# Conv 2's row terms in a tile of their own, added by an accumulating DMA, and its end rows evicted by ScalarE

## The chip, the cores and the metric

The kernel runs on one core of one Trainium2 chip. The metric is the device time of one execution in microseconds (us), as the median of several runs. Below, PE is the matrix engine (TensorE), PEld its weight load, DVE is VectorE, ACT is ScalarE, POOL is GpSimd and SP is SyncE. Each engine works through its own queue of instructions in order. DMAs are issued from the queues of SP (plain loads and stores) and POOL (those that add to their destination, and here the stores of conv 2). L730 means line 730 of the kernel before.

## The reference, cut to what matters

```python
def reference(x, t_emb, g1, be1, w1, w_emb, g2, be2, w2):   # x: (2, 512, 64, 64) bf16
    h = conv3(_silu(gn(x, g1, be1)), w1)                    # 3x3, 512 -> 512 channels
    emb = _silu(t_emb) @ w_emb
    h = h + emb.reshape(B, C, 1, 1)
    h = conv3(_silu(gn(h, g2, be2)), w2)
    return x + h
```

`gn` is a group norm with four groups of 128 channels. The last line matters here: the output of conv 2 has x added to it.

## The kernel before, in words

**Tiling.** Channels lie on the 128 partitions, in four tiles (`ct` for inputs, `ot` for outputs). A chunk is half an image (32 rows) of one of the two batches, so there are four chunks for each conv, and a *group* is one chunk and one output tile: 16 groups for conv 1 (layer 0), 16 for conv 2 (layer 1), `grp` 0 to 15 in each.

**Winograd by rows.** Four output rows are made from six input rows. A group therefore has six sums over 512 input channels, positions 0 to 5. Positions 0 and 5 (the *end rows*) are accumulated in PSUM tiles `acc` (pool `ps_acc`, two tiles). Positions 3 and 4 go to `mid`; positions 1 and 2 are transformed along the columns too and go to `nst` (nested; two tiles). `nst` and `mid` share the pool `ps_two` of three tiles. In the last chunk (`FOUR`) positions 1 to 4 are all nested. PE works through a group as nst, mid, acc.

**Inverse transform.** ScalarE evicts nst (`evac_nested`, L782) and mid (`evac_mid`, L797) to the tile `rm`, whose second half is `msl`, the four middle sums. `cols_mid` undoes the column transform on VectorE. `rows_mid` (L804 to L815) makes sums and differences of `msl` in `sts`, then the row terms: output rows 1 and 2 go straight to the output tile `yst` (seen as `y4`, four rows by `t`), and the parts of rows 0 and 3 that don't come from the end rows go to `tt`. Its three scalings by 8, 2 and 4 (L776 on ScalarE, L778 on VectorE) go where `ACT_SCALES` says: to ScalarE in conv 2's groups 0 to 11.

**Closing a group.** PE's end rows of group g are finished when group g+1 begins. So `close_group` of g is called within g+1, after the nested matmuls are queued: on VectorE one operation for each end row reads `acc`, scales it, adds `tt` and writes `yst` (L827; conv 1's groups 0 to 3 add `tt` on PE and evict on ScalarE, L821 and L830). Then `fin` stores. In conv 2's groups 0 to 13 (`by_dma`) `fin` issues two DMAs on POOL's queue: one that adds x from memory to `yst` (L843), and the store of `yst` (L844), which waits until the addition has landed. Groups 14 and 15 load x into the output tile by SP beforehand (`xr`, L686) and add it on VectorE. `yst` and `xr` come from the pool `stg`, tag `io`, three tiles in turn.

**What runs beside it.** `_Background` spreads the making of the next chunk's input V over the groups (`produce_V`: a Silu on ScalarE, L427, a copy scaled by -4, L433, then VectorE's additions, L442 to L491, through two tiles `ak`) and the transform of the weights (`prep_U`, L251, L254). For chunk 1 of conv 2 the addition of L442 is made by two accumulating DMAs from `ak` to `ak` on POOL's queue (L437). Group 3 of conv 2 also computes the scale and bias of the second group norm for batch 1 (`gn2_scale`): a small matmul (L165), a few tiny operations on VectorE (L167 to L189) and two on POOL (L179, and a `pow`, L186).

The framework draws each engine's order from the program's order, the dependences and a timing model of its own; at run time each queue keeps the order it was given.

Of the kernel before, what the change touches and what calls it, by code (L numbers as in the profile page):

```python
# [10 lines left out]
ALU = mybir.AluOpType  # L11
# [3 lines left out]
F16 = mybir.dt.float16  # L15
# [47 lines left out]
def kernel(  # L63
# [13 lines left out]
    nc = tc.nc  # L77
    P = nc.NUM_PARTITIONS
    B, C, H, W = x.shape
# [9 lines left out]
    TR = 8  # L89
    CR = TH * TR  # L90
# [6 lines left out]
    KAPPA = 1.0 / (6.0 * WS)  # L97
    ROWS_BY_DMA = lambda layer, b, ch: 4 * layer + 2 * b + ch in (5,)
    NFLAT = 2
    ACT_SCALES = lambda layer, grp: layer == 1 and grp < 12  # L100
    X_BY_DMA = lambda grp: grp < 14
    ROW = TR * WP
    VD, VN = 4 * ROW, NC * 2 * NHALF
# [7 lines left out]
    x_v = x.rearrange("b (ct p) h w -> b ct p (h w)", p=P)  # L111
# [48 lines left out]
    def flat(t):  # L160
        return t[:].rearrange("p r w -> p (r w)")
# [32 lines left out]
    def after(inst, dep):  # L194
        if dep is not None:
            tc.add_manual_dep(inst.ins, dep.ins.name, SYNC_DEP, reason="dma ordering")
        return inst

    def gram_pe(pieces, grf):
# [397 lines left out]
    st2 = {}  # L597
    pend = []
    deferred = []

    def aux_plan(layer, g):
        acts = []
# [25 lines left out]
    for layer in range(2):  # L628
        for idx, (b, ch) in enumerate(chunks):
            for ot in range(CT):  # L630
# [133 lines left out]
                raw = rm[:, 0].rearrange("p (a q t e w) -> p a q t e w", a=2, q=2, t=TR, e=2)  # L764
                msl = rm[:, 1].rearrange("p (s t w) -> p s t w", s=4, t=TR)
                tu = otmp.tile([P, 2, TR, 2, HALF], F16, tag="tu")
                sts = otmp.tile([P, 4, TR, W], F16, tag="sts")
                qs = otmp.tile([P, 2, TR, W], F16, tag="qs")
                if last_two == 1:
                    tt = srcp.tile([P, 2, TR, W], F16, tag="src", name="tt")  # L770
                else:
                    tt = otmp.tile([P, 2, TR, W], F16, tag="tt")

                def scaled(o, i, f, on_act=ACT_SCALES(layer, grp)):
                    if on_act:
                        nc.scalar.activation(out=o, in_=i, func=ACT.Copy, scale=f)  # L776
                    else:
                        nc.vector.tensor_scalar(out=o, in0=i, scalar1=f, scalar2=None, op0=ALU.mult)  # L778
# [21 lines left out]
                    if not first_evac:  # L800
                        first_evac.append(i_a)

                def rows_mid(scaled=scaled, add_x=layer == 1 and not by_dma, y4=y4, sts=sts, msl=msl, tt=tt, qs=qs):
                    nc.vector.tensor_tensor(out=sts[:, 2:4], in0=msl[:, 0:2], in1=msl[:, 2:4], op=ALU.add)  # L804
                    nc.vector.tensor_tensor(out=sts[:, 0:2], in0=msl[:, 0:2], in1=msl[:, 2:4], op=ALU.subtract)
                    nc.vector.tensor_tensor(out=tt[:, 0], in0=sts[:, 2], in1=sts[:, 3], op=ALU.add)
                    scaled(qs[:, 0], sts[:, 0], 8.0)
                    nc.vector.tensor_tensor(out=tt[:, 1], in0=qs[:, 0], in1=sts[:, 1], op=ALU.add)  # L808
                    if add_x:
                        nc.vector.tensor_tensor(out=tt[:], in0=tt[:], in1=y4[:, 0:4:3], op=ALU.add)  # L810
                    scaled(qs[:, 0], sts[:, 0], 2.0)
                    scaled(qs[:, 1], sts[:, 2], 4.0)
                    nc.vector.tensor_tensor(out=qs[:] if add_x else y4[:, 1:3], in0=sts[:, 1:4:2], in1=qs[:], op=ALU.add)  # L813
                    if add_x:
                        nc.vector.tensor_tensor(out=y4[:, 1:3], in0=qs[:], in1=y4[:, 1:3], op=ALU.add)  # L815

                def close_group(layer=layer, b=b, ch=ch, ot=ot, rows=rows, yst=yst, y4=y4, tt=tt, accs=accs,
                                ssum=ssum, ssq=ssq, on_dve=on_dve, by_dma=by_dma):
                    if not on_dve:
                        for k in range(2):  # L820
                            nc.tensor.matmul(accs[(0, 5)[k]], lhsT=id_end[:, k],  # L821
                                             rhs=tt[:, k].rearrange("p t (e w) -> p t e w", e=2), start=False, stop=True)
                    for k in range(2):
                        kw = {"accum_out": ssum[:, ch, k:k + 1]} if layer == 0 else {}
                        acc = accs[(0, 5)[k]].rearrange("p t e w -> p t (e w)")
                        if on_dve:
                            nc.vector.scalar_tensor_tensor(out=y4[:, (0, 3)[k]], in0=acc, scalar=(0.25, 1.0)[k],  # L827
                                                           in1=tt[:, k], op0=ALU.mult, op1=ALU.add, **kw)
                        else:
                            nc.scalar.activation(out=y4[:, (0, 3)[k]], in_=acc, scale=(0.25, 1.0)[k],  # L830
                                                 func=ACT.Identity if layer == 0 else ACT.Copy, **kw)

                    def fin():
                      if layer == 0:
                        yf = flat(yst)
                        nc.sync.dma_start(out=h_scr[b, ot][:, rows], in_=yf)
                        junk = otmp.tile([P, CR * W], F16, tag="sts", name="junk")
                        nc.scalar.activation(out=junk[:, 0:CR * W // 2].rearrange("p (f t w) -> p f t w", f=2, w=W),  # L838
                                             in_=y4[:, 1:3], func=ACT.Identity, accum_out=ssum[:, ch, 2:3])
                        nc.scalar.activation(out=junk[:], in_=yf, func=ACT.Square,  # L840
                                             scale=float(HW) ** -0.5, accum_out=ssq[:, ch:ch + 1])
                      elif by_dma:
                        nc.gpsimd.dma_start(out=flat(yst), in_=x_v[b, ot][:, rows], accum_op=ALU.add)  # L843
                        nc.gpsimd.dma_start(out=out_v[b, ot][:, rows], in_=flat(yst))  # L844
                      else:
                        nc.sync.dma_start(out=out_v[b, ot][:, rows], in_=flat(yst))
                    return fin
# [33 lines left out]
                if first_set:  # L881
                    for pos in DIRECT + NESTED:
                        open_acc(pos)
                    aux = None
                    for ct in range(CT):
                        if ct % 2 == 0:
                            aux = ps_two.tile([P, 2, NFREE], F32, tag="two", name="aux1")
                        gn1_load(ct)
                        gn1_stats(aux[:, ct % 2], ct)
                        for pos in DIRECT + NESTED:  # L890
                            for kx in KX_ORDER:
                                mm_direct(pos, ct, kx, ct == 0 and kx == KX_ORDER[0],
                                          (pos in (1, 2, 3, 4) or on_dve) and ct == CT - 1 and kx == KX_ORDER[-1])
                    evac_mid(0)
                    evac_mid()
                    for _ in range(3):
                        bg.tick()
                    rows_mid()
                    for _ in range(3):
                        bg.tick()  # L900
                    pend.append(close_group)
                else:
                    for pos in NESTED:
                        mms(pos)
                        bg.tick()
# [12 lines left out]
                    bg.tick()  # L918
                    mms(4)
                    bg.tick()  # L920
                    run_aux(layer, grp)
                    if four:
                        evac_nested(1)
                        cols_mid(1)
                    else:
                        evac_mid()
                    rows_mid()
                    if last_two == 0:
                        deferred.append((end_rows, close_group))
                    elif last_two == 1:  # L930
                        ends, close = deferred.pop()
                        ends()
                        close()()
                        close_halves()
                    else:
                        for pos in (0, 5):
                            mms(pos)
                            bg.tick()
                        pend.append(close_group)
# [41 lines left out]
```

## Time and profile before

| | us |
|---|---|
| median of 3 runs (lowest, highest) | 508.08 (506.97, 510.08) |
| the profiled execution | 509.58 |
| its span, first to last instruction | 507.8 |
| granted TensorE clock, mean | 0.978 |
| conv 2's first nested matmul starts at | 277.52 |

The page's second part shows the span in 40 slices of 12.7 us: a digit is the busy share in tenths, and PEclk the clock that PE was granted.

```profile
PE   4899999899999999999999999989999999999996
...
DVE  4789899999986994469999999768998999547776
ACT  4688899699965954478999899509779633333350
POOL 1210000100000000010011002221011101110100
PEclk9679999999999999999999999989999999999999
```

PE is busy nearly everywhere. Conv 2 is slices 22 to 40; VectorE and ScalarE are nearly full in the first of them, and ScalarE has room in the last ten or so.

### The profile page before, as it was taken

Reading aid. Unit: us, or ns where it says so; the run is one execution under the profiler, and the core shown is the slowest. Engines: PE = TensorE matmul, PEld = TensorE weight load, DVE = VectorE, ACT = ScalarE, POOL = GpSimd, SP = SyncE. Lnnn points to the kernel's source line nnn. Section 1 sums busy time; section 2 is a strip of 40 time slices with the busy share of each in tenths; the row PEclk is TensorE's granted clock in tenths of the full one; section 3 lists DMA queues with packets and bytes.
Section 4 is the critical chain, followed back from the end, with each engine's and each line's share of the span. In section 5 each row is a group of like instructions: output and inputs, shape, how many; then the busy total and the mean of one; then the engine's idle time right before and its main releaser. Section 6 shows DMA issues by size and latency. Waiting matters only on the chain. (4 is left out here: it accounts for less than half of the span.)

```text
span 507.8 us, 8116 instructions
## 1 busy us (share of the span) xinstructions
PE 486.2 (96%) x3140; PEld 285.8 (56%) x3140; DVE 426.1 (84%) x946; ACT 350.9 (69%) x341; POOL 44.1 (9%) x92
## 2 busy tenths in 40 slices
PE   4899999899999999999999999989999999999996
PEld 4865454555555555555555555545555555557784
DVE  4789899999986994469999999768998999547776
ACT  4688899699965954478999899509779633333350
POOL 1210000100000000010011002221011101110100
PEclk9679999999999999999999999989999999999999
DMA  8939231142431421133476334735554632325442
GB/s 309 365 110 333 80 119 64 45 158 92 118 95 53 142 74 43 41 121 109 152 199 178 105 87 112 155 84 130 123 134 119 124 74 55 94 71 124 122 87 83
DMA packets 24144, 61.99 MB, mean 122 GB/s; under 512 B 2219, under 2 KB 11563, under 8 KB 23723
## 3 DMA queue, kind: packets, MB, share of 16 engines
q1 hardware_dynamic: 18864, 44.64, 26.6%
q0 software_dynamic: 5184, 16.85, 15.2%
q8 instruction: 24, 0.39, 0.3%
q14 instruction: 13, 0.11, 0.1%
q10 hardware_dynamic: 59, 0.01, 0.0%
HBM read 42.54 MB, written 16.78 MB: 117 GB/s over the span
## 5 line engine op out<-in xcount | busy, mean ns | idle before, releaser
L730 PE MATMUL acc<-V,R 128*128 128x512 f16 x744 | 173.5, 390 | 3.4 <-DVE yst L827 2.6
L730 PE MATMUL mid<-V,U 128*128 128x512 f16 x720 | 167.2, 387 | 1.7 <-ACT rm L797 1.7
L730 PEld LDWEIGHTS <-R 128*128 128x128 bf16 x792 | 77.6, 99 | 95.6 <-issue 5.9
L730 PEld LDWEIGHTS <-U 128*128 128x128 f16 x720 | 70.2, 98 | 88.0 <-issue 5.3
L741 PE MATMUL nst<-V,U 128*128 128x256 f16 x1024 | 116.7, 273 | 0.0
L741 PEld LDWEIGHTS <-U 128*128 128x128 f16 x1056 | 103.3, 98 | 18.6
L782 ACT ACTIVATE rm<-nst 128x1024 f16<-128x1024 f32 x68 | 67.2, 1013 | 37.4 <-PE nst L741 24.7
L427 ACT ACTIVATE ak<-src,nb_all,sc_all 128x2112 f16<-128x2112 f16 (+1 forms) x28 | 59.9, 2143 | 9.3 <-DVE V L475 5.5
L433 ACT ACTIVATE ak<-ak 128x2112 f16<-128x2112 f16 x32 | 62.7, 1959 | 1.1 <-DVE V L473 0.4
L797 ACT ACTIVATE rm<-mid 128x1024 f16<-128x1024 f32 x30 | 30.4, 1015 | 27.3 <-PE mid L730 27.3
L776 ACT ACTIVATE qs<-sts 128x512 f16<-128x512 f16 x36 | 22.0, 626 | 28.8 <-DVE sts L804 22.9
L442 DVE TENSOR_TENSOR ak<-ak 128x2112 f16<-128x2112 f16 x28 | 34.9, 1250 | 5.7 <-ACT ak L433 5.7
L475 DVE TENSOR_TENSOR V<-ak 128x1056 f16<-128x1056 f16 x56 | 39.2, 700 | 0.3
L827 DVE SCALAR_TENSOR_TENSOR yst<-acc,tt 128x512 f16<-128x512 f32 x52 | 35.5, 683 | 1.8 <-PE acc L730 1.3
L789 DVE TENSOR_TENSOR tu<-rm 128x512 f16<-128x512 f16 x34 | 14.3, 419 | 24.8 <-ACT rm L782 24.6
L254 ACT ACTIVATE S<-R 128x1536 f16<-128x1536 bf16 (+1 forms) x28 | 31.4, 1155 | 2.7 <-DVE U L251 1.4
L838 ACT ACTIVATE junk<-yst 128x1024 f16<-128x1024 f16 x16 | 16.9, 1058 | 23.3 <-DVE yst L813 23.2
L840 ACT ACTIVATE junk<-yst 128x2048 f16<-128x2048 f16 x16 | 30.5, 1906 | 1.2 <-DVE yst L827 1.0
L251 DVE TENSOR_TENSOR U<-S 128x1536 f16<-128x1536 f16 x32 | 29.7, 948 | 0.0
L804 DVE TENSOR_TENSOR sts<-rm 128x1024 f16<-128x1024 f16 x32 | 21.9, 685 | 7.3 <-ACT rm L797 7.0
L491 DVE TENSOR_TENSOR V<-V 128x512 f16<-128x512 f16 x64 | 26.1, 431 | 0.0
L448 DVE TENSOR_TENSOR ak<-ak 128x1056 f16<-128x1056 f16 x32 | 22.5, 702 | 3.6 <-DMA ak<-ak 3.4
(124 smaller groups left out, 445.9 us busy)
## 6 DMA issues: line engine op xcount, KB each, us to landing
src<-h_scr SPq DMA_DIRECT2D x16, 528.0 KB, 4.1
h_scr<-yst SPq DMA_DIRECT2D x16, 512.0 KB, 2.7
yst<-in_x_dram POOLq DMA_DIRECT2D x14, 512.0 KB, 5.5
out_dram<-yst POOLq DMA_DIRECT2D x14, 512.0 KB, 3.0
src<-in_x_dram SPq DMA_DIRECT2D x12, 528.0 KB, 7.9
R<-in_w_dram SPq DMA_DIRECT2D x16, 384.0 KB, 4.2
xt<-in_x_dram SPq DMA_DIRECT2D x8, 512.0 KB, 5.9
g1t<-in_w_dram SPq DMA_DIRECT2D x16, 192.0 KB, 5.0
```

What stands on the lines that cost most here:

```text
L251: nc.vector.tensor_tensor(out=o, in0=i0, in1=i1, op=op)
L254: ts = lambda o, i, f: nc.scalar.activation(out=o, in_=i, func=ACT.Copy, scale=f)
L427: nc.scalar.activation(out=at[:, lo - r0:hi - r0, 1:W + 1], in_=sap, func=ACT.Silu, bias=nb_all[:, layer, b, ct:ct + 1], scale=sc_all[:, l ...
L433: nc.scalar.activation(out=diff, in_=same, func=ACT.Copy, scale=-4.0)
L442: nc.vector.tensor_tensor(out=diff, in0=diff, in1=below, op=ALU.add)
L475: nc.vector.tensor_tensor(out=pair(k).rearrange("p q (t w) -> p q t w", w=WP), in0=in0, in1=in1, op=op)
L730: nc.tensor.matmul(out, lhsT=w_direct(pos, ct, kx), rhs=rhs, start=first, stop=last)
L741: nc.tensor.matmul(accs["nst", (pos - 1) // 2][bank][:, q, :, plane, :], lhsT=lhsT, rhs=rhs.rearrange("p (t w) -> p t w", w=HALF), start=s ...
L782: nc.scalar.activation(out=raw[:, bank].rearrange("p q t e w -> p (q t e w)"), in_=accs["nst", k][bank][:].rearrange("p q t e w -> p (q t ...
L797: i_a = nc.scalar.activation(out=msl[:, 1 - k:4 - k:2].rearrange("p s t w -> p s (t w)"), in_=accs["mid", k][:].rearrange("p s t e w -> p ...
L827: nc.vector.scalar_tensor_tensor(out=y4[:, (0, 3)[k]], in0=acc, scalar=(0.25, 1.0)[k], in1=tt[:, k], op0=ALU.mult, op1=ALU.add, **kw)
L840: nc.scalar.activation(out=junk[:], in_=yf, func=ACT.Square, scale=float(HW) ** -0.5, accum_out=ssq[:, ch:ch + 1])
```

## The change

It concerns the 14 groups of conv 2 whose x is added by DMA, and has these parts:

- A new `rows_z` takes the place of `rows_mid` there. It writes the row terms of all four output rows into a tile `zt` of their own, laid out as the output tile is, and uses the output tile for intermediate values. Six additions of 512 elements and three scalings stand in place of two additions of 1024, two of 512 and one of 1024, and three scalings. There is one such tile (`otmp` has one buffer).
- ScalarE evicts both end rows of these groups into `yst` (the `else` branch with `nc.scalar.activation`), and VectorE no longer touches them.
- `fin` issues a DMA that adds `zt` to `yst`, then the store of the group *before*. The x addition of a group is issued in the next group, after that group's `rows_z` in the program, and its store one group later still. `behind` draws edges that only order the scheduling.
- The scalings go to ScalarE in conv 2's groups 2 to 13, instead of 0 to 11.
- `sts` and `tt` share a tile with `zt`; `qs` shares one with `tu`; in the last group `sts` takes a tile of the pool `src`.

```diff
-    ACT_SCALES = lambda layer, grp: layer == 1 and grp < 12
+    ACT_SCALES = lambda layer, grp: layer == 1 and 1 < grp < 14
...
+    ORDER_DEP = mybir.DependencyInfo(mybir.DependencyClass.NoSync, mybir.DependencyReason.SCHED_ONLY)
+
+    def behind(inst, dep):
+        if dep is not None:
+            tc.add_manual_dep(inst.ins, dep.ins.name, ORDER_DEP, reason="order")
+        return inst
...
+    def add_image(inst):
+        while to_add:
+            dst, src, y, zi = to_add.pop()
+            behind(behind(nc.gpsimd.dma_start(out=y, in_=src, accum_op=ALU.add), zi), inst)
+            to_store.append((dst, y))
+
+    def store_out(zi):
+        while to_store:
+            dst, y = to_store.pop()
+            behind(nc.gpsimd.dma_start(out=dst, in_=y), zi)
...
-                sts = otmp.tile([P, 4, TR, W], F16, tag="sts")
-                qs = otmp.tile([P, 2, TR, W], F16, tag="qs")
-                if last_two == 1:
+                if by_dma:
+                    zt, sts, tt = otmp.tile([P, TR, 4, W], F16, tag="st", name="zt"), None, None
+                elif last_two == 1:
+                    zt = None
+                    sts = srcp.tile([P, 4, TR, W], F16, tag="src", name="sts")
                     tt = srcp.tile([P, 2, TR, W], F16, tag="src", name="tt")
                 else:
-                    tt = otmp.tile([P, 2, TR, W], F16, tag="tt")
+                    zt = None
+                    st = otmp.tile([P, 6, TR, W], F16, tag="st")
+                    sts, tt = st[:, 0:4], st[:, 4:6]
...
+                def rows_z(scaled=scaled, y4=y4, msl=msl, zt=zt):
+                    z = zt[:].rearrange("p t s w -> p s t w")
...
+                    tt_(y4[:, 0], msl[:, 0], msl[:, 2], ALU.subtract)
+                    scaled(z[:, 3], y4[:, 0], 8.0)
+                    tt_(y4[:, 3], msl[:, 0], msl[:, 2])
+                    scaled(y4[:, 1], y4[:, 0], 2.0)
+                    scaled(y4[:, 2], y4[:, 3], 4.0)
+                    tt_(z[:, 1], msl[:, 1], msl[:, 3], ALU.subtract)
+                    tt_(z[:, 2], msl[:, 1], msl[:, 3])
+                    tt_(z[:, 0], y4[:, 3], z[:, 2])
+                    return tt_(z[:, 3], z[:, 3], z[:, 1])
...
-                        if on_dve:
+                        if on_dve and not by_dma:
...
-                        nc.gpsimd.dma_start(out=flat(yst), in_=x_v[b, ot][:, rows], accum_op=ALU.add)
-                        nc.gpsimd.dma_start(out=out_v[b, ot][:, rows], in_=flat(yst))
+                        zi = nc.gpsimd.dma_start(
+                            out=flat(yst), in_=zt[:].rearrange("p t f w -> p (t f w)"), accum_op=ALU.add)
+                        store_out(zi)
+                        to_add.append((out_v[b, ot][:, rows], x_v[b, ot][:, rows], flat(yst), zi))
...
-                    rows_mid()
+                    add_image(rows_z() if by_dma else rows_mid())
+                    if last_two >= 0:
+                        store_out(None)
```

More of the change, by code (lines that the diff above doesn't have):

```diff
@@ L599 @@
     deferred = []
+    to_add = []
+    to_store = []
+    def add_image(inst):
[7 more added lines that the diff above has]
+            behind(nc.gpsimd.dma_start(out=dst, in_=y), zi)
     def aux_plan(layer, g):
@@ L801, in evac_mid, with tt_, rows_mid @@
                         first_evac.append(i_a)
-                def rows_mid(scaled=scaled, add_x=layer == 1 and not by_dma, y4=y4, sts=sts, msl=msl, tt=tt, qs=qs):
+                def rows_z(scaled=scaled, y4=y4, msl=msl, zt=zt):
+                    z = zt[:].rearrange("p t s w -> p s t w")
+                    def tt_(o, i0, i1, op=ALU.add):
+                        return nc.vector.tensor_tensor(out=o, in0=i0, in1=i1, op=op)
+                    tt_(y4[:, 0], msl[:, 0], msl[:, 2], ALU.subtract)
[7 more added lines that the diff above has]
+                    return tt_(z[:, 3], z[:, 3], z[:, 1])
+                def rows_mid(scaled=scaled, add_x=layer == 1 and not by_dma, y4=y4, sts=sts, msl=msl, tt=tt):
+                    qs = otmp.tile([P, 2, TR, W], F16, tag="tu", name="qs")
                     nc.vector.tensor_tensor(out=sts[:, 2:4], in0=msl[:, 0:2], in1=msl[:, 2:4], op=ALU.add)
@@ L812, in rows_mid @@
                     scaled(qs[:, 1], sts[:, 2], 4.0)
-                    nc.vector.tensor_tensor(out=qs[:] if add_x else y4[:, 1:3], in0=sts[:, 1:4:2], in1=qs[:], op=ALU.add)
+                    inst = nc.vector.tensor_tensor(
+                        out=qs[:] if add_x else y4[:, 1:3], in0=sts[:, 1:4:2], in1=qs[:], op=ALU.add)
                     if add_x:
-                        nc.vector.tensor_tensor(out=y4[:, 1:3], in0=qs[:], in1=y4[:, 1:3], op=ALU.add)
+                        inst = nc.vector.tensor_tensor(out=y4[:, 1:3], in0=qs[:], in1=y4[:, 1:3], op=ALU.add)
+                    return inst
                 def close_group(layer=layer, b=b, ch=ch, ot=ot, rows=rows, yst=yst, y4=y4, tt=tt, accs=accs,
-                                ssum=ssum, ssq=ssq, on_dve=on_dve, by_dma=by_dma):
-                    if not on_dve:
+                                ssum=ssum, ssq=ssq, on_dve=on_dve, by_dma=by_dma, zt=zt):
+                    if not on_dve and not by_dma:
                         for k in range(2):
@@ L836, in fin @@
                         nc.sync.dma_start(out=h_scr[b, ot][:, rows], in_=yf)
-                        junk = otmp.tile([P, CR * W], F16, tag="sts", name="junk")
+                        junk = otmp.tile([P, CR * W], F16, tag="st", name="junk")
                         nc.scalar.activation(out=junk[:, 0:CR * W // 2].rearrange("p (f t w) -> p f t w", f=2, w=W),
```

## The prediction

> **What bounds the kernel now.** I read the page's busy line first, then the PE timeline of conv 2, then the waits and queues around each place where PE loses time.
>
> ```profile
> PE 486.2 (96%) x3140; PEld 285.8 (56%) x3140; DVE 426.1 (84%) x946; ACT 350.9 (69%) x341; POOL 44.1 (9%) x92
> ```
>
> PE is the bound, and the change leaves every matmul as it is. So the gain can only be PE time that conv 2 loses to others. The PE timeline (start, length, what, idle before in brackets) has two losses with an idle gap of a µs or more:
>
> ```profile
> 320.04 3.66 PE L741 MATMUL nst<-V,U 128*128 128x256 f16 x32
> 323.53 5.50 PE L730 MATMUL mid<-V,U 128*128 128x512 f16 x24
> 328.87 0.28 PE L165 MATMUL aux<-me,ones_neg 128*128 128x8 f32 x2
> 331.77 7.13 PE L730 MATMUL acc<-V,R 128*128 128x512 f16 x24 [2.61 <-DVE yst L827]
> 338.74 3.66 PE L741 MATMUL nst<-V,U 128*128 128x256 f16 x32
> ...
> 382.10 3.66 PE L741 MATMUL nst<-V,U 128*128 128x256 f16 x32
> 386.82 5.50 PE L730 MATMUL mid<-V,U 128*128 128x512 f16 x24 [1.06 <-ACT rm L797]
> ```
>
> An undisturbed group takes 14.17 us from nst to nst (397.49 to 411.67). Group 3 of conv 2 takes 338.74 - 320.04 = 18.70; 0.14 of it is its aux matmul (in conv 1 a group with one took 14.31), so **4.39 us** are lost: 2.61 idle, and then 24 matmuls in 7.13 instead of 5.50, at a granted clock of 0.88 in that window. Group 6 (367.12 to 382.10) loses **0.81** and group 7 (382.10 to 397.49) **1.22**. Sum 6.42 us. That is the ceiling of the gain, 1.26%.
>
> **Why group 3 stalls.** POOL's queue there (start, length, what, the wait before it):
>
> ```profile
> 319.61 0.87 POOL L437 DMA_DIRECT2D ak<-ak  x1 [2.12 <-ACT ak L433]
> 324.32 0.56 POOL L844 DMA_DIRECT2D out_dram<-yst  x1 [3.85 <-DMA yst<-in_x_dram]
> 324.88 0.90 POOL L437 DMA_DIRECT2D ak<-ak  x1
> ...
> 339.15 0.56 POOL L844 DMA_DIRECT2D out_dram<-yst  x1 [4.92 <-DMA yst<-in_x_dram]
> 339.73 0.25 POOL L179 TENSOR_SCALAR var<-var 128x4 f32<-128x4 f32 x1
> ```
>
> And DVE's:
>
> ```profile
> 328.98 0.71 DVE L448 TENSOR_TENSOR ak<-ak 128x1056 f16<-128x1056 f16 x1 [3.45 <-DMA ak<-ak]
> ...
> 331.03 0.68 DVE L827 SCALAR_TENSOR_TENSOR yst<-acc,tt 128x512 f16<-128x512 f32 x1
> ```
>
> POOL works in order. Its store waits 3.85 us for the x addition before it, and the second half of the `ak` addition stands behind that store. DVE then waits 3.45 us for that half, and group 2's end rows, whose PSUM tiles PE wants, stand behind DVE's wait. A second chain starts here: the `pow` of GN2 for batch 1 (L179) stands behind another store, so ScalarE begins the activations of the next V at 343.22. From 350 to 378 DVE is busy 13.9 of every 14 us and ACT 11.4 and 12.8; groups 6 and 7 stall because ACT's eviction of mid stands behind a Silu that waited 2.07 and 2.39 us for DVE.
>
> **The change, part by part.** The rows that price it (busy us, mean ns | idle before):
>
> ```profile
> L827 DVE SCALAR_TENSOR_TENSOR yst<-acc,tt 128x512 f16<-128x512 f32 x52 | 35.5, 683 | 1.8 <-PE acc L730 1.3
> L830 ACT ACTIVATE yst<-acc 128x512 f16<-128x512 f32 x8 | 4.7, 590 | 0.8 <-PE acc L821 0.8
> L776 ACT ACTIVATE qs<-sts 128x512 f16<-128x512 f16 x36 | 22.0, 626 | 28.8 <-DVE sts L804 22.9 <-DVE tt L808 5.4 <-DVE sts L805 0.2
> L806 DVE TENSOR_TENSOR tt<-sts 128x512 f16<-128x512 f16 x32 | 13.3, 416 | 0.0
> ```
>
> *DVE.* A group used 0.685 + 0.682 + 0.416 + 0.415 + 0.684 (L804, L805, L806, L808, L813) + 2 x 0.683 (L827) = 4.25 us. `rows_z` has six 512-element operations of 0.416 = 2.50: 1.75 less in groups 2 to 11. Groups 0 and 1 add three scalings on DVE (0.283 each, L778): 3.35, 0.9 less. Groups 12 and 13 lose such scalings: 2.6 less. Outputs in runs of 64 elements cost nothing extra: L813 already writes such runs at 0.684 for 1024.
>
> *ACT.* Two evictions of 0.590 (L830) = 1.18 more in groups 2 to 11; in 0 and 1 three scalings of 0.626 go, so 0.70 less; in 12 and 13 it is 1.18 + 1.88 = 3.06 more, where ACT is busy 4 to 6 us in 14.
>
> *z addition.* One more accumulating DMA in each of 14 groups, 512 KB from SBUF to SBUF, not in the trace. Nearest: the x addition, as large (0.88 us to issue; landing 5.4 to 7.4, median 5.5), and `ak`, half as large (3.3 to 5.7). I take 0.9 + 5.5 = 6.4; bounds 4.2 and 8.3, no gain possible. In one group: end rows done at 0, two evictions 1.2, landed at 7.6; `rows_z` of the next group writes the single z tile at about 10 (mid ends at 8.83, eviction 1.0). Slack 2.3 us: with the upper bound, 9.5, it still fits when ACT is on time. If not, ScalarE's scaling into z (DVE's in groups 0 and 1) waits, and behind it in ACT's queue stand evictions of nst and mid, which PE needs 8 to 9 us after it has filled them. So up to 8 us of lateness costs nothing in an easy group, but in groups 4 to 7, where the eviction of mid is already that late, it counts one for one. In 380 to 400, two additions and two stores took 40.9% of 20 us of the engines, 4.1 us a pair; the extra addition is under that, and adds at most 0.29 to a DMA share that is 0.29 to 0.67 in conv 2. It fits.
>
> The Trainium skill ("DMA: Bandwidth & Descriptors", Anatomy of one DMA, SWDGE path) fits such a DMA as 2.0 us plus bytes over 436 GB/s, an estimate of 3.2 us for 512 KB; the row says 5.5 and decides. By the rule the slack would be 4.6 us instead of 2.3, and the sum below the same.
>
> A rule against the change: the skill ("SBUF — State Buffer", the "DVE blocks DMA" trap) says that GpSimd cannot write descriptors while VectorE holds the port they share, and gives 620 ns growing to 3100. Here the x addition took POOL 862 to 940 ns in all 14 cases beside a busy DVE, so no such growth shows; by the rule each z addition would land some 2.5 us later and the slack would be gone.
>
> *POOL's order.* By the code, group 3 now queues z(2), store(1), then the `pow`, then x(2). So the `pow` no longer stands behind an x addition that itself waits for group 2's end rows. It can follow var on DVE (336.89, earlier once DVE is relieved); the 4.1 us that DVE waited for POOL at 341.14 can go. The z addition waits for ACT alone. Against it: one more wait stands in POOL's queue per group, and `ak` additions queue there until 325.
>
> *Group 3, −4.39.* End rows no longer pass through DVE's queue; ACT is free at 320.1 and waited 11.84 us for DVE later, so it evicts well before 329. What is late next is V for group 4: in the trace its last operation ends at 334.98, of which L813 and two L827 (1.8 us) now go: 333.2, against a PE that wants it at 334.35. It fits by 1.1 us if the `ak` half lands as now.
>
> *Groups 6 and 7, −2.03 at most.* PE now comes 4.4 us earlier, so ACT's queue must too; V for group 8 itself is no bound (done at 382.4 for a start at 397.49). ACT's run from 343.22 to the eviction at 385.77 held some 5.5 us of waits; 3.3 groups x 1.18 = 3.9 us of new work enter, and DVE gives 3 x 1.75 = 5.2 back. If the `pow` frees the start by the 4.1 us, ACT starts that eviction at about 385.8 − 4.1 − (5.5 − 3.9) = 380.1 and ends it at 381.1; PE wants it at 386.82 − 1.06 − 5.2 = 380.6 (5.2 are the losses before it). So with no wait left it is 0.5 us late, and with three of the 5.5 us of waits left 3.5. I put 1.4 us of loss here, nearer the lower end, because DVE gets back more (5.2) than ACT takes (3.9).
>
> *Stores a group later.* io has three tiles. A store of group g would go out early in g+2, and the tile is next written 10 us into g+3: hidden. The x loads of groups 14 and 15 wait for stores 11 and 12. Store 12 follows x addition 12, landed by 487; + 0.6 + 3.0 + 5.9 (512 KB of x, row xt) = 496.5, wanted at 499.3: hidden, 2.8 us of cover, zero to +2 at the end.
>
> *Conv 1* keeps its arithmetic; its scaled rows share a tile with `tu`, both on DVE in order, and the junk tile overlaid `sts` already: 0, between −1 and +1.
>
> **Sum.** −6.42 + 1.4 = −5.0 us. The profiled execution took 509.58 (span 507.8 and 1.8 around it): 504.6 from it. The three runs have a median of 508.08, 1.5 less, so I forecast **503.1 us**.
>
> **The rivals.** *(N) The gain at group 3 is given back in groups 4 to 7*: ACT, with 1.18 us more a group, becomes the late one there, or the `pow` starts no earlier. For it: ACT's 11.4 and 12.8 of 14. Against: its waits for DVE. Then 4.39 + 2.03 shrink to 0 to 3: 505 to 508, about 506.5.
>
> *(S) Slower: POOL's queue in groups 2 and 3.* If the second `ak` half stands behind a z and an x addition, 2 x 6.4 = 12.8 us instead of today's 4.4, V for group 4 is ready at 333.2 + 8.4 = 341.6, 2.9 us later than PE began it; with a cold restart (+1.63) and 6 and 7 unrelieved that is +4.5: 512.6. It costs from a delay of 5.5 us on (338.74 − 333.2). For it: POOL's waits of 3.85 to 6.15 us at every store. Against: the z addition waits for nothing on DVE's queue but rows long done. Three landings before the `ak` half, 19.2 instead of 4.4, would make it 348.0 and 519. V for group 8 adds nothing: its last operation (L491) ends at 382.4, 15 us before PE wants it.
>
> *(M) The change does not do what it says*: ACT's evictions are queued behind scalings that wait for DVE, and group 3 stalls as before: 508, within N.
>
> **How the numbers follow.** Forecast case (501.7 to 505) 0.54, N and M 0.20, S 0.26. A measurement of this kernel tells about 1%, 5.1 us, from no change. Under 503.0 needs at most 1.3 us of the losses left: with the forecast at 1.4, some 0.32 of its 0.54, since the ways to be better are bounded by the floor 1.3 us below and the ways to be worse end in N. Of S, 0.18 lies over 513.2, from a delay of 9 us on. So faster 0.32, slower 0.18, same 0.50 (0.22 + 0.20 + 0.08). The floor is 508.08 − 6.42 = 501.7; with the runs' spread of a us below the median, 501.0 is the low end. Up to 515 leaves out the heavier half of S, about 0.14. The forecast case's own range is 501.5 to 505.
>
> **What would show it.** Right: no gap before acc at group 3, groups 3, 6 and 7 at 14.2 to 15.4 us, DVE at about 426 − 24 = 402 us busy, ACT at 367, the `pow` before 339. Wrong: a PE wait for V (L475, L491) at the start of group 4 or 8; an ACT wait on the z addition followed by a PE wait on `rm`; the last x load landing after 499.

## The result and the profile after

Before: 508.53 us, the median of six runs (506.97 to 510.08). After: **502.26 us**, six runs (500.42 to 503.72). The ratio of after to before is 0.9883, with a 95% interval of 0.9861 to 0.9904. The profiled execution took 503.72 us against 509.58, spans 501.9 and 507.8.

The busy line of the page after:

```profile
PE 482.8 (96%) x3140; PEld 283.9 (57%) x3140; DVE 403.8 (80%) x932; ACT 362.3 (72%) x369; POOL 56.2 (11%) x106
```

PE has the same 3140 matmuls. DVE is 22.3 us less busy, ACT 11.4 more, POOL 12.1 more. None of this moves the end by itself; that is read from the matmuls. The timeline of PE in conv 2 after the change (start, length, what, idle before in brackets), groups 1, 3 and the start of 4:

```profile
291.04 3.66 PE L761 MATMUL nst<-V,U 128*128 128x256 f16 x32
295.77 5.50 PE L750 MATMUL mid<-V,U 128*128 128x512 f16 x24 [1.07 <-ACT rm L821]
...
320.62 3.66 PE L761 MATMUL nst<-V,U 128*128 128x256 f16 x32
324.12 5.50 PE L750 MATMUL mid<-V,U 128*128 128x512 f16 x24
329.46 0.28 PE L165 MATMUL aux<-me,ones_neg 128*128 128x8 f32 x2
329.60 5.50 PE L750 MATMUL acc<-V,R 128*128 128x512 f16 x24
334.93 3.66 PE L761 MATMUL nst<-V,U 128*128 128x256 f16 x32
```

Group 3 takes 14.31 us: no gap before acc, and acc in 5.50 us instead of 7.13. Groups 4 to 11 take 14.17 or 14.18 each, so groups 6 and 7 lose nothing either (12 and 13, in the last chunk, take 12.33, as before). One loss is new: 1.07 us of idle before mid of group 1, which takes 15.41 (1.24 lost). From the first nst of conv 2 to its last matmul PE needs 221.07 us (276.87 to 497.94) where it needed 226.29 (277.52 to 503.81): 5.22 less. Below, this is "the conv 2 time"; without any loss it would be 219.87.

POOL's queue after, from the store that is issued in group 2 (store 0) to the `pow` of group 3 (start, length, what, the wait before it):

```profile
317.85 0.57 POOL L619 DMA_DIRECT2D out_dram<-yst  x1 [3.61 <-DMA yst<-in_x_dram]
319.08 1.78 POOL L444 DMA_DIRECT2D ak<-ak  x2 [0.65 <-ACT ak L440]
...
328.13 0.86 POOL L886 DMA_DIRECT2D yst<-zt  x1 [6.27 <-ACT yst L873]
328.71 0.85 POOL L619 DMA_DIRECT2D out_dram<-yst  x1
334.31 0.23 POOL L179 TENSOR_SCALAR var<-var 128x4 f32<-128x4 f32 x1 [4.75 <-DVE var L178]
```

Both halves of the `ak` addition are issued together at 319.08; before, the second stood behind a store until 324.88. The `pow` starts at 334.31 instead of 339.73, and what it waits for is now var on DVE. Store 1 follows z(2) without a wait, because it no longer stands right behind the x addition of its own group. DVE and ScalarE at the same place, then ScalarE at group 1 and at the next V:

```profile
325.94 0.71 DVE L455 TENSOR_TENSOR ak<-ak 128x1056 f16<-128x1056 f16 x1 [2.34 <-DMA ak<-ak]
326.57 0.42 DVE L831 TENSOR_TENSOR zt<-yst,zt 128x512 f16<-128x512 f16 x1
```

```profile
290.79 2.14 ACT L434 ACTIVATE ak<-src,nb_all,sc_all 128x2112 f16<-128x2112 f16 x1
...
294.72 1.01 ACT L821 ACTIVATE rm<-mid 128x1024 f16<-128x1024 f32 x1
...
324.88 0.58 ACT L873 ACTIVATE yst<-acc 128x512 f16<-128x512 f32 x1
327.10 0.60 ACT L873 ACTIVATE yst<-acc 128x512 f16<-128x512 f32 x1 [1.65 <-DVE zt L831]
...
337.84 2.13 ACT L434 ACTIVATE ak<-src,nb_all,sc_all 128x2112 f16<-128x2112 f16 x1
```

DVE still waits 2.34 us for the second `ak` half. The second end-row eviction (327.10) waits 1.65 us for DVE: it writes the plane of the output tile that `rows_z` has used for a sum, and DVE reads that sum at 326.57, behind its own wait. It is done at 327.70 and PE wants the PSUM tile at 329.60: a cover of 1.9 us. The first Silu of the next V begins at 337.84, which is 2.91 us after PE began group 4; before it was 4.48 (343.22 − 338.74). In group 1 a Silu (290.79) stands ahead of the eviction of mid (294.72), and PE waits for that one. ScalarE had also been held up before that, by DVE's last reading of `S`, the one buffer for scaled weights:

```profile
283.35 1.82 DVE L258 TENSOR_TENSOR U<-S 128x1536 f16<-128x1536 f16 x2
285.25 2.22 ACT L261 ACTIVATE S<-R 128x1536 f16<-128x1536 bf16 x2 [2.47 <-issue]
```

The view names no releaser for these 2.47 us; but DVE's reading ends at 285.17, and ScalarE writes the same buffer 0.08 us later.

### The profile page after: what moved, and what is told of

It is laid out like the page before. It is cut to its first block, busy times and chain, and to the rows that moved or that the text cites. A ratio compares the mean times of both kernels' runs of the same rounds, so it can differ in the third digit from the quotient of the medians.

```text
span 501.9 us, 8180 instructions
## 1 busy us (share of the span) xinstructions
PE 482.8 (96%) x3140; PEld 283.9 (57%) x3140; DVE 403.8 (80%) x932; ACT 362.3 (72%) x369; POOL 56.2 (11%) x106
## 4 chain that ended last, share of the span: by engine, by line
PE 68%; DVE 17%; DMA 6%; ACT 5%; issue 3%; POOL 1%; DVEq 0%; SPq 0%; ACTq 0%
PE acc L750 24%; PE mid L750 21%; PE nst L761 18%; DMA xt<-in_x_dram 3%; DVE U L258 3%; DMA xbuf<-in_x_dram 2%; DVE S L258 1%; DVE V L482 1%; PE ga L209 1%; DVE ak L449 1%; PE aux L209 1%; DVE U L236 1%; PE half L750 1%; DMA R<-in_w_dram 1%; DVE V L498 1%
## 5 line engine op out<-in xcount | busy, mean ns | idle before, releaser
L800 ACT ACTIVATE zt<-yst 128x512 f16<-128x512 f16 x12 | 7.5, 628 | 23.7 <-DVE yst L831 23.7
L873 ACT ACTIVATE yst<-acc 128x512 f16<-128x512 f32 x36 | 20.2, 589 | 6.1 <-issue 3.4
L815 DVE TENSOR_TENSOR rm<-tu,rm 128x1024 f16<-128x1024 f16 x34 | 23.3, 686 | 0.6 <-ACT rm L806 0.2
```

## The experiments

Four questions were open: what removed group 3's stall, whether the z addition costs anything, what decides the loss in groups 4 to 7, and where group 1's loss comes from. "Start" in the table is the first Silu of the next V minus PE's start of group 4; "4 to 7" is the time that these four groups lose. Times are medians, and each ratio is to runs of the kernel before on the same chip (their medians are 507.6 to 508.5); the last five columns are read from one profiled execution of each kernel.

| kernel | us | ratio, 95% interval | conv 2 time | group 1 | group 3 | start | 4 to 7 |
|---|---|---|---|---|---|---|---|
| before | 508.53 | 1 | 226.29 | 0 | 4.39 | 4.48 | 2.05 |
| after | 502.26 | 0.9883 (0.9861 to 0.9904) | 221.07 | 1.24 | 0 | 2.91 | 0 |
| e1_stores_late | 506.26 | 0.9962 (0.9945 to 0.9980) | 224.27 | 0 | 0.62 | 6.20 | 3.79 |
| e2_ends_on_dve | 507.54 | 0.9994 (0.9980 to 1.0008) | 225.57 | 1.24 | 0.64 | 5.93 | 3.85 |
| e3_all_at_once | 513.82 | 1.0110 (1.0082 to 1.0139) | 230.13 | 1.20 | 5.28 | 7.50 | 3.81 |
| e4_pe_adds | 514.12 | 1.0129 (1.0103 to 1.0154) | 232.96 | – | – | – | – |
| e5_scales_on_dve | 502.00 | 0.9892 (0.9866 to 0.9919) | 221.00 | 1.16 | 0 | 2.18 | 0 |
| e6_late_gn2_early | 504.33 | 0.9942 (0.9920 to 0.9965) | 223.23 | 0 | 0.68 | −8.3 | 0.76 |
| e7_less_act | 501.93 | 0.9893 (0.9866 to 0.9920) | 220.53 | 0 | 0 | 4.39 | 0.70 |
| e8_no_z | 501.59 | 0.9886 (0.9862 to 0.9910) | 221.01 | 1.18 | 0 | 1.66 | 0 |
| e10_stores_behind | 503.85 | 0.9924 (0.9902 to 0.9947) | 223.26 | 0 | 2.29 | 3.52 | 1.12 |
| e11_both | 501.78 | 0.9884 (0.9863 to 0.9906) | 220.58 | 0 | 0 | 4.29 | 0.73 |
| e12_no_edges | 511.74 | 1.0079 (1.0058 to 1.0101) | 230.34 | 1.19 | 6.60 | 6.38 | 2.70 |
| e13_dve_from_3 | 503.81 | 0.9901 (0.9866 to 0.9937) | 221.40 | 1.16 | 0 | 2.47 | 0.40 |

**e1_stores_late**: the kernel before, with nothing changed but the place of the store in the program.

```diff
                         nc.gpsimd.dma_start(out=flat(yst), in_=x_v[b, ot][:, rows], accum_op=ALU.add)
-                        nc.gpsimd.dma_start(out=out_v[b, ot][:, rows], in_=flat(yst))
+                        store_out()
+                        to_store.append((out_v[b, ot][:, rows], flat(yst)))
```

> The kernel before with one part of the change alone: the store of a group is queued on POOL one group later; end rows stay on VectorE, no z tile. POOL's queue then holds both halves of the last ak addition ahead of any store. Theory P (the stall of group 3 comes from POOL's order: store, then ak half): VectorE's wait of 3.45 us for ak shrinks below 2.5, group 3 loses under 1.5 us instead of 4.39, total 503.5 to 505. Theory A (what counts is that end rows leave VectorE's queue): group 3 still loses 3 us or more, total 506.5 to 509.

Group 3's loss fell from 4.39 to 0.62, with the end rows still on DVE and no z tile: in this trace both `ak` halves are issued at 318.18, ahead of the store (322.99). But the store of the next group still stands ahead of the `pow`, which begins at 336.28 after a wait of 5.00 us for the x landing. The planner had put each store back behind its own x addition, since nothing tied it to the next group. Groups 4 to 7 then lost 3.79 us, 1.74 more than before the edit, so nearly half of the 3.77 gained at group 3 was given back, and the total missed the 503.5 to 505 that theory P expected.

**e10_stores_behind**: the same, but store g − 1 is tied by an order-only edge behind the x addition of group g, as the change ties its own.

```diff
-                        store_out()
+                        xi = nc.gpsimd.dma_start(out=flat(yst), in_=x_v[b, ot][:, rows], accum_op=ALU.add)
+                        store_out(xi)
...
+                tc.add_manual_dep(st.ins, xi.ins.name, ORDER_DEP, reason="order")
```

> The kernel before with late stores and the ordering edge of the change: the store of group g-1 is held behind the x addition of g on POOL (without the edge, in e1_stores_late, the scheduler hoisted it back to where it waits for a landing, ahead of the pow). End rows stay on VectorE, no z tile. Theory T (groups 5 to 7 keep up if the first Silu of the next V starts under 3 us after PE's group 4): the pow follows var, the Silu starts 2.5 to 3.5 us after group 4's first matmul (e1: 6.2, changed kernel: 2.9), groups 5 to 7 lose under 1 us, conv 2 takes 220.5 to 221.5 us of PE time as in the changed kernel, total 502 to 504. Theory D (VectorE must get time back, so the z tile is needed): groups 5 to 7 still lose 2.5 us or more, total 505 to 507.

The order alone gives 0.76% of the 1.17%. The `pow` came at 334.73 and groups 4 to 7 lost 1.12, between what theories T and D expected. Group 3 lost 2.29 here: the store (315.19) now travels beside the `ak` halves (317.59), DVE waits 3.01 us for the second half instead of 1.34 in e1, and the end rows stand behind that wait.

**e2_ends_on_dve**: the kernel after, its end rows evicted by DVE.

```diff
+                        elif by_dma:
+                            nc.vector.tensor_scalar(out=y4[:, (0, 3)[k]], in0=acc, scalar1=(0.25, 1.0)[k],
+                                                    scalar2=None, op0=ALU.mult)
```

> The changed kernel with one part undone: end rows of the 14 groups are evicted by VectorE (a scaling out of PSUM, about 0.68 us each) instead of ScalarE; z addition and late stores stay. Theory A: group 3's stall is back by 2.5 us or more and the total is 505 to 508. Theory P: POOL's order is the good one, group 3 loses under 1.5 us and the total is 501.5 to 504; ScalarE, with 1.18 us a group less, has no stall in group 1.

With z, the edges and the late stores, but the end rows back on DVE, the whole gain is gone in the total (ratio 0.9994), though group 3 keeps all but 0.64 of it. Var is late on DVE, so the `pow` comes at 336.13 and the first Silu 5.93 us after PE's group 4; groups 4 to 7 lose 3.85. Here the z transfer is no longer free for DVE: with the end rows later, the z addition is issued later, and DVE waits 2.47 us (321.40) and 1.38 us (334.60) for z landings before it can write the z tile again. Theory P was right on group 3 and missed the total (501.5 to 504) and group 1, which still loses 1.24. With the late stores in place, ScalarE's eviction is thus not what cures most of group 3; it cures the last 0.64 here and brings the next V's start forward.

**e3_all_at_once** and **e12_no_edges**: the kernel after with POOL's order taken away. e3 queues z addition, x addition and store of a group in one go; e12 keeps the program text and drops the edges alone.

```diff
-                        store_out(zi)
-                        to_add.append((out_v[b, ot][:, rows], x_v[b, ot][:, rows], flat(yst), zi))
+                        nc.gpsimd.dma_start(out=flat(yst), in_=x_v[b, ot][:, rows], accum_op=ALU.add)
+                        nc.gpsimd.dma_start(out=out_v[b, ot][:, rows], in_=flat(yst))
```

```diff
     def behind(inst, dep):
-        if dep is not None:
-            tc.add_manual_dep(inst.ins, dep.ins.name, ORDER_DEP, reason="order")
         return inst
```

> The changed kernel with one part undone: z addition, x addition and store of a group are queued one behind the other as soon as its end rows are evicted. Theory A: group 3 loses under 1 us; total 501.5 to 503.5. Theory P: the pow of GN2 for batch 1 stands behind store 2, which waits for two landings (about 6 us each) after the eviction, so it runs at 339 to 342 instead of 334.6; the Silu of the next V starts 4 to 6 us later than 337.8, and groups 5 to 7 lose 1 to 4 us; total 503 to 507.

> The changed kernel without its ordering edges and nothing else changed: the scheduler puts each group's x addition and store straight behind its z addition, as in e3_all_at_once. Theory T: the pow is at 341 or later, the first Silu starts 6 us or more after group 4's first matmul, group 3 loses 4 to 5.5 us and groups 4 to 7 another 3 to 4: 509 to 514, slower than before. Theory A (end rows on ScalarE suffice): 502 to 505.

Both are slower than before, and e3 is slower than either of its theories expected. Without its edges the planner gave e12 the same order on POOL as e3. POOL's queue of e12 around group 3:

```profile
311.62 1.06 POOL L884 DMA_DIRECT2D yst<-zt  x1
320.17 0.87 POOL L611 DMA_DIRECT2D yst<-in_x_dram  x1 [7.50 <-DMA yst<-zt]
320.72 2.14 POOL L442 DMA_DIRECT2D ak<-ak  x2
326.04 0.56 POOL L617 DMA_DIRECT2D out_dram<-yst  x1 [3.18 <-DMA yst<-in_x_dram]
```

and its ScalarE and PE there:

```profile
329.64 0.60 ACT L871 ACTIVATE yst<-acc 128x512 f16<-128x512 f32 x1 [4.62 <-DVE zt L829]
```

```profile
331.20 0.60 PE L165 MATMUL aux<-me,ones_neg 128*128 128x8 f32 x2 [3.50 <-ACT rm L804]
331.65 8.13 PE L748 MATMUL acc<-V,R 128*128 128x512 f16 x24
```

The x addition now waits 7.50 us at the head of POOL's queue for the landing of z, and the `ak` halves stand behind it. DVE waits 5.30 us for them, ScalarE's second end-row eviction waits 4.62 us for DVE's last read of the plane it writes, and the eviction of nst (L804) behind it keeps PE idle for 3.50 us and it restarts slowly: 8.13 us for the 24 matmuls that take 5.50, at a granted clock of 0.66 in that stretch. So the end rows are on ScalarE and group 3 still loses 6.60, more than before the change. Work and transfers of e12 are those of the kernel after: the edges alone are worth 9.5 us (511.74 − 502.26), 9.3 of it in the conv 2 time.

**e8_no_z**: the kernel after without the z addition's transfer; the row terms are missing from its output.

```diff
-                        zi = nc.gpsimd.dma_start(
-                            out=flat(yst), in_=zt[:].rearrange("p t f w -> p (t f w)"), accum_op=ALU.add)
+                        zi = None
```

> The changed kernel without the z addition itself (the row terms are computed into z and left there, so the output lacks them): POOL has 14 DMAs less, and nobody waits for z. If the addition is hidden, as forecast: the time of the changed kernel within 1 us (501.3 to 503.3), no change in PE's groups. If it costs through ScalarE's and VectorE's waits or through the DMA engines: 1.2 us or more faster, group 1's stall gone.

221.01 against 221.07 for the conv 2 time, and medians that cannot be told apart (501.59 and 502.26): in this kernel the transfer is hidden, all 14 of it.

**e4_pe_adds**: the kernel before with the other place for the same addition: ScalarE evicts the end rows, and PE adds the row terms to the accumulator by two more matmuls a group.

```diff
-    DVE_ENDS = [(0, g) for g in range(4, 16)] + [(1, g) for g in range(0, 16)]
+    DVE_ENDS = [(0, g) for g in range(4, 16)] + [(1, g) for g in range(14, 16)]
```

> The kernel before, with ScalarE evicting the end rows of conv 2's groups 0 to 13 and PE adding tt to acc by two more matmuls a group (as in conv 1's groups 0 to 3); no z tile, no later store. PE's work grows by 28 x 0.222 = 6.2 us. Theory A: group 3's gap goes, but PE now waits for tt itself, so 6.2 comes on top of 501.7 to 504: 508 to 510. Theory P: the ak wait on VectorE stays, tt of group 2 is no later than its end rows were, and PE waits for tt: 511 to 515.

An undisturbed group takes 14.60 instead of 14.17, and group 1 takes 20.19: PE waits 0.75 for the row terms from DVE and 2.98 for ScalarE's end-row evictions (301.01), which stand behind scalings of the next weights. Moving the addition onto the engine that bounds the kernel costs its full price, and adds a new wait. Group 3 loses nothing here with POOL's old order, but this does not decide what cures its stall: PE comes to group 3's end rows 6.9 us later than in the kernel before, counted from conv 2's first matmul, and DVE's wait for `ak` ends only 2.3 us later.

**e5_scales_on_dve, e6_late_gn2_early, e13_dve_from_3**: what decides the loss in groups 4 to 7? One explanation (T in the expectations) is how late the first Silu of the next V starts; another (D) is DVE's load there, 51.96 us busy in these four groups before and 43.35 after. ScalarE's load (C) is no candidate: it is 47.34 us before and 49.12 after, where nothing is lost. e5 is the kernel after with the scalings of groups 4 to 7 back on DVE. e6 is e1 with the statistics of GN2 for batch 1 closed a group earlier. e13 is the kernel after with the end rows of groups 3 to 13 on DVE, so that from group 4 on it has the loads of e2 but keeps the early start.

```diff
-    ACT_SCALES = lambda layer, grp: layer == 1 and 1 < grp < 14
+    ACT_SCALES = lambda layer, grp: layer == 1 and (1 < grp < 4 or 7 < grp < 14)
```

```diff
-            if g == 3:
+            if g == 2:
                 acts.append(lambda k: gn2_scale(k[0], 1))
```

```diff
+                        elif by_dma and grp > 2:
+                            nc.vector.tensor_scalar(out=y4[:, (0, 3)[k]], in0=acc, scalar1=(0.25, 1.0)[k],
+                                                    scalar2=None, op0=ALU.mult)
```

> The changed kernel with the three scalings of conv 2's groups 4 to 7 on VectorE (0.28 us each) instead of ScalarE (0.63 each): VectorE gets back 0.9 us a group against the kernel before instead of 1.75, ScalarE loses 0.7 instead of gaining 1.18. Theory D (groups 5 to 7 keep up because VectorE got time back): 0.5 to 2 us are lost again in groups 4 to 7; total 502.8 to 504.5. Theory C (ScalarE's load decides there): no loss there; total at or under that of the changed kernel, 501 to 502.5.

> The kernel before with late stores (as e1_stores_late) and GN2's scale for batch 1 computed in group 2 instead of 3; end rows stay on VectorE, no z tile. Theory T (groups 5 to 7 stall because the Silus of the next V start late, at 65.7 us after conv 2's start before and 63.7 with late stores): they start 2 to 10 us earlier, the losses of groups 5 to 7 fall from 3.8 us to under 1, total 502 to 504. Theory D (VectorE has no time there, wherever it starts): they keep 2.5 us or more; total 505 to 507.

> The kernel after, with the end rows of conv 2's groups 3 to 13 evicted by VectorE (two operations of 0.68 us a group), those of groups 0 to 2 still by ScalarE. From group 4 on each engine then has the load of the version whose end rows all went to VectorE, which began the activations of the next V 5.93 us after PE began group 4 and lost 3.85 us of PE time in groups 4 to 7; but here nothing is changed before the `pow` of group 3, so they should begin about 2.9 us after PE began group 4, as in the kernel after. If the loss in groups 4 to 7 follows from that start alone, they lose 0 to 0.6 us and the time is 502 to 503. If it follows from VectorE's load, they lose 3 us or more as in that version, and the time is 505 to 506. A loss of 1 to 2 us would mean that both count. Group 1 should lose 1.2 and group 3 nothing by either.

e5 lost nothing with part of the relief taken back. e6, with none of the relief, lost 0.76 in groups 4 to 7 where e1 lost 3.79; its aux matmul, now in group 2, waited 1.68 us for an eviction there, and group 2 took 2.09 longer (0.14 of it the aux matmul itself). e13 and e2 have the same operations on the same engines from group 3's end rows on and differ in the start, 2.47 against 5.93, and lose 0.40 and 3.85; the later Silus of e2 come 3.3 to 3.5 us after those of e13 as well. The start decides most of it. The load is not without weight: e7 and e11 start as late as before (4.39 and 4.29 against 4.48) with DVE relieved (in e11 in part) and lose 0.7 instead of 2.05. In these 13 kernels (e4 left out), a start up to 3 us after PE's group 4 loses 0 to 0.8, one of 3.5 to 4.5 loses 0.7 to 2.05, and one of about 6 and more loses 2.7 to 3.9.

**e7_less_act, e11_both**: group 1. e7 is the kernel after with one of ScalarE's weight pieces of conv 2 scaled by DVE; e11 adds e5's edit to it.

```diff
-... + [(1, o, q) for o in range(4) for q in range(2)]
+... + [(1, o, q) for o in range(4) for q in range(2) if (o, q) != (1, 1)]
```

> The changed kernel with one weight piece of conv 2 (output tile 1, second pair) scaled on VectorE (about 1.6 us) instead of ScalarE (3.8 us), which comes at the end of conv 1. ScalarE then evicts mid of group 0 ahead of the Silu that stood before it. If group 1's 1.24 us is ScalarE being late: it vanishes, total 501 to 501.5. If VectorE, full there, becomes late instead: a loss of 1 us or more appears in groups 0 to 3 or V for group 4 is late; total 502.5 to 505.

> The changed kernel with both relocations that cost nothing: the weight piece of e7_less_act on VectorE and the scalings of groups 4 to 7 on VectorE. e7 lost 0.38 and 0.33 us in groups 5 and 6, where e5_scales_on_dve lost nothing; so conv 2 should take 219.9 to 220.5 us of PE time against 221.1 in the changed kernel; total 501 to 502. If VectorE becomes late, groups 5 to 7 lose 1 us or more and the total is 502.5 or above.

Group 1's loss is gone. ScalarE's timeline of e7 there:

```profile
288.82 1.00 ACT L821 ACTIVATE rm<-mid 128x1024 f16<-128x1024 f32 x1
...
297.04 2.17 ACT L434 ACTIVATE ak<-src,nb_all,sc_all 128x2112 f16<-128x2112 f16 x1
```

The eviction of mid begins 1.95 us after that of nst (286.87), and the Silu stands 8 us behind it, as it stands behind it in the kernel before (eviction 291.87, Silu 297.90). In the kernel after the Silu had moved ahead of the eviction. The edit changed the load and the order together, but the traces tell them apart: ScalarE takes up its weight scalings 9.15 us after conv 2's first matmul in e7 (283.28, after a wait of 4.53 us for DVE's reading of `S`) and 8.38 us after it in the kernel after (285.25). So e7 is not ahead in work, and what it gains is the order. In the kernel after, the eviction ends 1.07 us too late, less than the Silu's 2.14 us or the 2.47 us of the wait for `S`; by this sum, an estimate, either one gone would have been enough. The gain is 0.5 us of conv 2 time, since PE, now earlier, loses 0.7 in groups 4 to 7. The medians of e7 and e11, 501.93 and 501.78, cannot be told from 502.26; no version measured here beats the change clearly.

## Why the prediction was right, and where it was not

Forecast 503.1, measured 502.26. In the conv 2 time the forecast was −6.42 + 1.4 = −5.0; it came out at −6.42 + 1.24 = −5.2. That the loss left over is so close in size is luck, as the groups below show. The medians differ by 6.3, and by the interval of the ratio 4.9 to 7.1, so no further term is shown. The sum fits, but some of its steps were not as written.

**Group 3, −4.39: right in size, half wrong in cause.** "End rows no longer pass through DVE's queue" does not hold. The second end-row eviction writes a plane that `rows_z` uses as scratch, and so it still waits for DVE: 1.65 us in the kernel after, 4.62 in e12. The scalings ahead of the evictions waited for DVE too (3.72 us at 323.31). So rival M's mechanism is real. What makes it harmless is POOL's order, which the prediction counted under the `pow` and not under group 3: both `ak` halves are issued ahead of the x addition (319.08), so that DVE's wait ends at 325.94 instead of 328.98. With the order alone group 3 loses 0.62 (e1) or 2.29 (e10), with ScalarE's eviction and no order 5.28 and 6.60 (e3, e12), with both 0. One reading of the prediction is off: the granted clock of 0.88 is that of 322 to 336, and in the 7.13 us of the 24 matmuls it was 0.76.

**POOL's order: right.** The forecast sequence z(2), store(1), `pow`, x(2) is the one in the trace. The `pow` was to come before 339, and came at 334.31, led by var on DVE. V for group 4 is ready at 331.1 (forecast 333.2).

**Rival S: right on POOL's queue, not on how that reaches PE; absent here.** Its order (the `ak` halves behind z and x additions) is the one that e3 and e12 have. It was priced at +4.5 (512.6), and they took 513.82 and 511.74; but S let PE wait for V of group 4, ready at 341.6, whereas in e12 that V is ready at 333.6 and PE loses its time earlier, behind ScalarE's evictions. So the match in price is luck. The point left unsaid in the prediction is what kept this order out: not the waits themselves but the edges.

**Rival N: not here, but in e2,** where groups 4 to 7 give the gain back (507.54, for a forecast of 505 to 508).

**Groups 6 and 7, "1.4 us of loss here": the step that failed.** They lost nothing. The size was about right for the sum, but the loss sits in group 1 (1.24), which the prediction took as free, as ScalarE has 0.70 us less to do in groups 0 and 1. The count was of work, and the loss came from the order in ScalarE's queue, together with its wait for DVE at 285.25. For groups 6 and 7 the estimate was a start of the activations 4.1 us earlier and 3 of 5.5 us of waits left. The start came 5.4 earlier (337.84 for 343.22; 4.7 counted from conv 2's first matmul), and in the run from there only two waits for V were left, 1.35 and 0.35 us at 357.19 and 370.69. ScalarE begins group 6's eviction of mid at 378.44 and ends it 1.5 us before PE's mid of group 7 (380.95).

**The z addition: right, and mis-sized on the safe side.** 4.6 us to landing (median of 14; 4.5 to 7.0) instead of 5.5, and 0.86 to issue instead of 0.9. DVE waited for a z landing four times, 4.5 us in all; e8 shows that this costs nothing. The Trainium skill ("DMA: Bandwidth & Descriptors", Anatomy of one DMA, SWDGE path) fits 2.0 us plus bytes over 436 GB/s, an estimate of 3.2 us for its size; no landing here was under 4.5, so for this accumulating transfer the measurement decides against it.

**Stores a group later: hidden, as forecast,** with more cover than forecast. Store 12 is issued at 475.09, behind z(13), and not after an x addition landed by 487; the last x load is issued at 480.49, and DVE adds it at 494.7 without a wait.

**Busy times:** DVE 403.8 (forecast 402), ACT 362.3 (forecast 367; I counted 16.5 more, it was 11.4). The count added up the records; in the trace the sum of ScalarE's records does rise by 17.1, but neighbouring records overlap by some 0.1 us, and busy time counts the overlap once.

## What to carry to other kernels

On an engine that works in order, the wait of one queued transfer delays everything behind it: before pricing a new DMA on such a queue, write down the order in which it and its neighbours will stand, and say what holds that order. Here the same transfers cost 511.7 us without order edges and 502.3 with them, while the 512 KB a group that were added cost nothing that shows. When a stall is removed, compare the next start with the bounding engine's need for it, and look at the order in the queue of the engine that took over the work: a lower count of work there does not exclude a new wait.

## What was not expected of the hardware

- **A transfer lands later beside another one.** Store landings, by the lists of DMA issues (each line's last figure is the median us to landing), in the kernel after and in e12:

```profile
out_dram<-yst POOLq DMA_DIRECT2D x14, 512.0 KB, 5.4
```

```profile
out_dram<-yst POOLq DMA_DIRECT2D x14, 512.0 KB, 3.0
```

  In e12 a store starts when the x addition before it has landed; in the kernel after most start 0.56 us behind the issue of another addition, and in e10, where the same holds without z, they take 6.2. The `ak` half goes from 4.2 (before) to 5.2. PE was hit by this in e10 alone, where DVE's wait for `ak` grew. The Trainium skill ("DMA: Bandwidth & Descriptors", Issuing engines are not separate DMA queues) says that all DMAs run on the same 16 engines and interleave; these rows agree, for two transfers of one issuer.
- **Issuing a plain store on POOL in the kernel after takes 0.57 us after a wait and 0.85 to 0.89 right behind another DMA** (317.85 and 328.71 above; the two records then overlap, with starts 0.56 apart).
- **Beside a busy DVE, POOL issued the 14 z additions in 851 to 882 ns each.** The Trainium skill ("SBUF — State Buffer", the "DVE blocks DMA" trap) says that GpSimd cannot write descriptors while VectorE runs an operation in a mode with two ports; none of the 14 issues was held up. Whether any VectorE operation here ran in such a mode, no run shows.
- **An idle time without a named releaser can be a plain wait for a buffer.** The 2.47 us of ScalarE at 285.25 stand in the trace as `issue`. In e7 the wait at the same place has a name, a DVE operation on U (4.53 us; DVE ends at 283.25, ScalarE starts at 283.28), and it is the same operation, the last to read `S`, that ends 0.08 us ahead of ScalarE in the kernel after.
